# Attention into a gated feed-forward block: two matrix products interleaved, sums moved between engines

## The chip, the cores and the metric

The kernel runs on one core of a Trainium2 chip. A core has TensorE (matrix products, written to the accumulation banks called PSUM), VectorE (elementwise work), ScalarE (tabulated functions and copies), GpSimd (elementwise work on SBUF, and the issue of many transfers) and SyncE (the issue of other transfers). The engines run at the same time and wait for each other by semaphores; each works through its own instructions in the order in which they were written. The metric is the device time of one execution in microseconds.

## The reference

The inputs are q, k and v of 8 batches, 8 heads, 576 positions and a head size of 64, all in float32, and two weight matrices of 512 by 2048 and 2048 by 512. The attention pools keys and values by eight positions; the feed-forward block multiplies each hidden value by its own cosine.

```python
k_p = k.reshape(B, H, Sp, 8, D).mean(axis=3)      # Sp = 72
v_p = v.reshape(B, H, Sp, 8, D).mean(axis=3)
scores = scale * np.matmul(q, k_p.transpose(0, 1, 3, 2))
scores = scores - np.max(scores, axis=-1, keepdims=True)
attn = np.exp(scores)
attn = attn / (np.sum(attn, axis=-1, keepdims=True) + 1e-09)
x = heads_joined(np.matmul(attn, v_p))            # 4608 tokens x 512
h = x @ w_in                                      # 4608 x 2048
g = h * np.cos(h)
out = g @ w_out                                   # 4608 x 512, float32
```

## The kernel before

The 4608 tokens are worked on in nine tiles of 512, numbered t = 0 to 8, one after the other. A tile first goes **up**: eight pairs of 128 hidden columns, for each pair a bank pair of PSUM that takes eight matmuls (`up_mm`, L353), a cosine on ScalarE (L363) and a product on VectorE (L367) that writes `g_sb` and so frees the bank. From tile 1 on the pairs are taken in the order 0, 4, 1, 5, 2, 6, 3, 7, in banks 0, 2, 1, the two output banks, 0, 2, 1, 0. Then the tile goes **down**, to `out`. While it does, the attention of the next batch, b = t + 1, is computed in the gaps: scores (L233), the exponential on ScalarE (L240), the values and the row sums (L268, L295), the division on VectorE (L279, L298, L300) and transposes by SyncE's queue into `xT` (L304). A batch has 576 positions and a tile 512, so the last 64 positions of a batch (`REST`) are done in the next tile.

The down projection of tile 0 is the plain one, 64 matmuls of 512 columns (L370). From tile 1 on it is a two-by-two block scheme with seven products instead of eight (`down_products`), each of 16 matmuls of 256 columns (L431). It needs sums of parts of g, called g1 to g4 (`put_g`, L397, on VectorE, each in two halves i = 0 and 1), and sums of parts of the output weights, called w1 to w4 (`put_weights`, L387, in two halves). Two output banks take the products in turn: products 0, 2, 4 and 6 go to one (A) and 1, 3 and 5 to the other (B); in the last tile each bank is a pair in separate places. After each product VectorE reads the bank (`each`: L445 for p1, the plain copy of product 0; L447 for the sums of a bank with an earlier copy). The next product of the same bank may start only after this read. From tile 7 on (t >= B - 1) the plain copy is on ScalarE.

The eight weight sums are made once, in tile 0: w1 of half 0, and w3, w2 and w4 of half 1, on VectorE; w3, w2 and w4 of half 0 and w1 of half 1 on GpSimd (L710 and L711), behind the issue of the loads for batch 2. On GpSimd's queue these are followed by the pooling of the keys and values of batch 2, which GpSimd does by three rounds of additions (`pool_first`, L156, and `pool_rest`, L162, L165 and L168), with the loads for the batch after in between.

The order around the change is written out by hand (`manual_schedule`): the order of the lines is the order on each engine. In tile 0 a list `fill` gives pairs of a matmul number and a piece of attention that is put in front of that matmul. In later tiles the sums of g for half 0 are put between the up pairs (L580), the sums of half 1 behind the first two products (L668 and L672). At the end of a tile GpSimd waits at a gate (L714), a copy of one element of g4, before it begins the next batch's pooling.

For the first stretch of a down projection these lines give the order:

```python
product(0)
product(1, 0, 2)
scores_of(u0, u1, u2)      # three score blocks, then three exponentials
product(1, 2)
put_gs((1, 1), (2, 1))
reads[0]()                 # p1: the copy of bank A, product 0
put_gs((3, 1), (4, 1))
reads[1]()                 # bank B, product 1
values_rows(*u0)
product(2)                 # bank A again; reads g2 and w2
```

Of the kernel before, what the change touches and what calls it, by code (L numbers as in the profile page):

```python
# [20 lines left out]
def kernel(  # L21
# [377 lines left out]
    def put_gs(*kis):  # L399
        for k, i in kis:  # L400
            put_g(k, i)

    def down_products(t):

        def of(w, m=0):
            return lambda fc: w[fc // 4][:, fc % 4, m * HM:(m + 1) * HM]

        def part(x):
            return lambda fc, p: x[:, fc, p * 128:(p + 1) * 128]

        apart = t == NT - 1
        if apart:
            A, Bb = [[x[:, 0:HM] for x in two] for two in (obanks, (banks[1][:, 0, :], banks[2][:, 0, :]))]
        else:
            A, Bb = [[obanks[i][:, p * HM:(p + 1) * HM] for p in range(2)] for i in (1, 0)]
        products = [
            (A, True, part(g_part(0, 0, 0, HF)), of(w_out_sb[0:2])),
            (Bb, True, part(g_part(1, 0, 0, HF)), of(w_out_sb[2:4])),
            (A, True, part(g2), of(w2)),
            (Bb, True, part(g1), of(w1)),  # L420
            (A, False, part(g3), of(w3)),
            (Bb, False, part(g4), of(w_out_sb[2:4], 1)),
            (A, False, part(g_part(1, 1, 0, HF)), of(w4)),
        ]
        mms = []
        for n, (bank, first, g, w) in enumerate(products):
            order = [(fc, p) for fc in range(HF) for p in range(2)]
            if apart and n == 6:
                order.sort(key=lambda x: x[1])
            for fc, p in order:  # L430
                mms.append(lambda bank=bank, first=first, g=g, w=w, fc=fc, p=p: nc.tensor.matmul(  # L431
                    bank[p], lhsT=g(fc, p), rhs=w(fc),
                    start=(first and fc == 0 and (apart or p == 0)), stop=(fc == HF - 1 and (apart or p == 1)),
                    skip_group_check=not first))

        p1, v16, q15 = [msb.tile([128, 2, HM], FP32, name=n, tag=n, bufs=1) for n in ("p1_sb", "v_sb", "q_sb")]
        o1, o2 = [msb.tile([128, 2, d_model], FP32, name="o_two", tag="o_two", bufs=2) for _ in range(2)]
        m1, m2 = slice(0, HM), slice(HM, d_model)

        def each(out, bank, other=None, m=slice(0, HM), tk=None):  # L440

            for p in range(2) if apart else (slice(0, 2),):
                ps = bank[p] if apart else obanks[1 if bank is A else 0].rearrange("p (a m) -> p a m", a=2)
                if other is None:
                    (nc.scalar.copy if t >= B - 1 else nc.vector.tensor_copy)(out=out[:, p, m], in_=ps)  # L445
                else:
                    nc.vector.tensor_tensor(out=out[:, p, m], in0=ps, in1=other[:, p], op=ADD)  # L447
                if apart and tk is not None:
                    rows_out(t, tk, out, (p,), m, (nc.sync, nc.scalar))

        reads = [
            lambda: each(p1, A),
            lambda: each(o1, Bb, p1, m1, 0),
            lambda: each(v16, A, p1),
            lambda: each(q15, Bb, p1),
            lambda: each(o2, A, q15, m2, 1),
            lambda: (each(o1, Bb, v16, m2, 0), apart or stores.append(lambda: rows_out(t, 0, o1))),
            lambda: (each(o2, A, p1, m1, 1), apart or stores.append(lambda: rows_out(t, 1, o2))),
        ]
        return [mms[i * 2 * HF:(i + 1) * 2 * HF] for i in range(7)], reads  # L460
# [100 lines left out]
    for t in range(NT):  # L561
# [5 lines left out]
        for n, fp in enumerate(up_order(t)):  # L567
            up_mm(t, fp, 2 if n < 2 else 0)
            between = ()
            if t == 0:  # L570
                if fp == 4:
                    puts = pool_k_mm(1, obanks[0], 0, 2), pool_k_mm(1, obanks[1], 2, 4)
                elif fp in (5, 6):
                    g0 = 9 * (fp - 5)
                    puts = q_transpose_mm(1, obanks[0], g0, g0 + 5), q_transpose_mm(1, obanks[1], g0 + 5, g0 + 9)
                if fp in (4, 5, 6):
                    puts[0](vec)
                    between = ((puts[1], act),)
            up_g(t, fp, between)
            if 0 < t and 3 <= n < 6:  # L580
                put_gs(*[(k, 0) for k in (((3,), (1,), ()) if t == 1 else ((1, 2), (3,), (4,)))[n - 3]])
            if 0 < t and b < B:
                if n == 0:
                    q_transpose(b)
                    k_transpose(b)
                elif n == 2:
                    pool_rest(b, "v")
                    if b + 1 < B:
                        nc.gpsimd.tensor_copy(out=gate, in_=kk[b % 2][0:1, H - 1, 0:1])
                        load_q(b + 1)  # L590
                        load_kv(b + 1, "v", v)
            if n == 2:
                while stores:
                    stores.pop(0)()
# [17 lines left out]
            fill = [(1, lambda: scores(t, REST, banks[2])), (16, lambda: values(t, REST, banks[1]))]  # L612
        if t == 0:
            fill = [(2, fill[0][1]), (2, S_(0, 0)), (8, lambda: pool_v_mm(1, banks[1])),
                    (8, lambda: values(t, REST, banks[2])), (8, S_(1, 0)), (8, V_(0, 1)),
                    (18, S_(2, 2)), (21, V_(1, 0, later)), (26, S_(3, 1)), (32, lambda: later.pop()()),
                    (32, V_(2, 2)), (40, V_(3, 0))]
        if t == FIRST:
            early_inverses.clear()
# [14 lines left out]
        else:  # L634
# [21 lines left out]
            steady, rest = b < B, t < B  # L656
            if rest:
                exp_tables()
            product(0)
            product(1, 0, 2)  # L660
            if steady:
                scores_of(u0, u1, u2)
            elif rest:
                scores_of(ur)
            product(1, 2)
            if t == 1:
                put_g(2, 0)
            put_gs((1, 1), (2, 1))  # L668
            reads[0]()
            if not steady:  # L670
                reads[1]()
            put_gs((3, 1), (4, 1))  # L672
            if steady:
                reads[1]()
                values_rows(*u0)
            if t == 1:
                put_g(4, 0)
            product(2)
            reads[2]()
            if steady:  # L680
# [24 lines left out]
        if b + 1 < B:  # L705
            if t == 0:
                load_kv(b + 1, "k", k)
                load_q(b + 1)
                load_kv(b + 1, "v", v)
                put_weights(0, nc.gpsimd, (3, 2, 4))  # L710
                put_weights(1, nc.gpsimd, (1,))  # L711
            else:

                nc.gpsimd.tensor_copy(out=gate, in_=g4[0:1, HF - 1, 0:1])  # L714
            pool_first(b + 1, "k")
            if t != 1 and b + 2 < B:
                load_kv(b + 2, "k", k)
            pool_rest(b + 1, "k")
            if t == 1:
                load_kv(b + 2, "k", k)  # L720
            pool_first(b + 1, "v")
# [28 lines left out]
```

The softmax here doesn't subtract the row's maximum and nothing guards it: scores larger than these inputs give would overflow.

## Time and profile before

| What | Time |
| --- | --- |
| Five runs, median | 286.54 us |
| Five runs, lowest and highest | 285.9 and 287.77 us |
| The profiled execution | 286.72 us |
| Its span | 284.9 us |
| TensorE busy in it | 276.3 us |
| VectorE busy | 215.3 us |
| ScalarE busy | 164.4 us |
| GpSimd busy | 143.8 us |
| Mean granted TensorE clock | 1.0 of full speed |

The profile is of one execution. Its span runs from the first to the last instruction on the core; the device time around it is a little longer. A row of a timeline gives the start in microseconds, the busy time, the engine, the line of the kernel, the operation with what it writes and reads, and how many instructions were merged; a bracket at its end gives the idle time ahead of it and what ended that. Instructions of one engine overlap a little, so that ends and starts cross. PE is TensorE, DVE VectorE, ACT ScalarE, POOL GpSimd and SP SyncE.

### The profile page before, as it was taken

The numbers are of one execution on the slowest core, as the hardware profiler recorded it, in microseconds if no ns is written. First come the engines' busy times: TensorE is split into PE (matmuls) and PEld (weight loads), VectorE is DVE, ScalarE is ACT, GpSimd is POOL, SyncE is SP. The second block draws the span as 40 slices with busy tenths as digits, with TensorE's granted clock in tenths as the row PEclk, the third lists the DMA queues.
The fourth block names the chain that finished last, engine by engine and source line by source line (L and its number), as shares of the span: only waits on it lengthen the run. The fifth ranks groups of instructions, "written<-read, shape, count | busy, mean of one in ns | idle before, by whom it ended". The sixth has DMA issues, their size and how long they took to land.

```text
span 284.9 us, 5857 instructions
## 1 busy us (share of the span) xinstructions
PE 276.3 (97%) x2360; PEld 176.5 (62%) x2360; DVE 215.3 (76%) x314; ACT 164.4 (58%) x193; POOL 143.8 (50%) x150
## 2 busy tenths in 40 slices
PE   7889999999999999999999999999999999999994
PEld 2545554446874587459745884588458844874583
DVE  5448757899957995699569956995699569856972
ACT  3787798367257735674566556655656555436600
POOL 8453169997599259934993499439900000000000
PEclk9999999999999999999999999999999999999999
DMA  7999999793939698898678968882670252015014
GB/s 147 194 206 208 206 205 220 123 204 50 148 45 170 124 217 139 132 171 164 104 136 154 181 96 154 145 175 55 117 157 3 55 123 45 0 24 126 2 37 111
DMA packets 57737, 36.12 MB, mean 127 GB/s; under 512 B 35440, under 2 KB 53360, under 8 KB 57712
## 3 DMA queue, kind: packets, MB, share of 16 engines
q0 software_dynamic: 19744, 18.07, 41.1%
q1 hardware_dynamic: 37328, 17.18, 29.4%
q10 hardware_dynamic: 640, 0.52, 0.8%
q8 instruction: 18, 0.29, 0.4%
q14 instruction: 7, 0.06, 0.1%
HBM read 36.70 MB, written 9.44 MB: 162 GB/s over the span
## 4 chain that ended last, share of the span: by engine, by line
PE 86%; DVE 6%; ACT 3%; DMA 2%; issue 1%; POOL 0%; DVEq 0%; POOLq 0%; ACTq 0%
PE bank L353 35%; PE obank L431 32%; PE obank L370 4%; PE obank L353 4%; PE bank L233 3%; DVE g_sb L367 3%; DMA q_b<-in_q_dram 2%; PE bank L295 2%; PE bank L431 2%; PE bank L268 1%; DVE w L387 1%; DVE g L397 1%; ACT cos L363 1%; ACT ex L240 1%; DVE vz L187 0%
## 5 line engine op out<-in xcount | busy, mean ns | idle before, releaser
L353 PE MATMUL bank<-xT,w_in_sb 128*128 128x512 bf16 x512 | 114.0, 379 | 0.2 <-DVE g_sb L367 0.2
L363 ACT ACTIVATE cos<-bank,half_pi 128x1024 f32<-128x1024 f32 x64 | 70.4, 1114 | 56.9 <-PE bank L353 55.0
L353 PEld LDWEIGHTS <-w_in_sb 128*128 128x128 bf16 x576 | 56.1, 98 | 66.2 <-issue 0.9
L367 DVE TENSOR_TENSOR g_sb<-bank,cos 128x1024 bf16<-128x1024 f32 x64 | 77.1, 1219 | 25.1 <-ACT cos L363 24.9
L156 POOL TENSOR_TENSOR half_sums<-kv_st 72x512 f32<-72x512 bf16 x48 | 54.8, 1168 | 0.6 <-issue 0.2
L240 ACT ACTIVATE ex<-bank 72x1024 bf16<-72x1024 f32 (+1 forms) x40 | 35.0, 929 | 34.0 <-PE bank L233 33.8
L431 PEld LDWEIGHTS <-g 128*128 128x128 bf16 x512 | 47.9, 98 | 6.2 <-issue 0.3
L431 PE MATMUL obank<-w,g 128*128 128x256 bf16 x368 | 42.7, 272 | 0.2 <-DVE p_sb L445 0.2
L431 PEld LDWEIGHTS <-g_sb 128*128 128x128 bf16 x384 | 36.8, 98 | 6.9 <-DVE g_sb L367 0.3
L162 POOL TENSOR_TENSOR half_sums<-half_sums 72x512 f32<-72x512 f32 x24 | 30.5, 1290 | 0.0
L431 PE MATMUL obank<-w_out_sb,g_sb 128*128 128x256 bf16 x240 | 28.9, 273 | 0.0
L397 DVE TENSOR_TENSOR g<-g_sb 128x1024 bf16<-128x1024 bf16 x32 | 23.3, 729 | 0.5
L714 POOL COPY gate<-g 1x1 bf16<-1x1 bf16 x5 | 0.9, 181 | 34.5 <-DVE g L397 34.5
L279 DVE TENSOR_TENSOR xT<-bank,inv 64x256 bf16<-64x256 f32 x14 | 5.9, 422 | 15.0 <-ACT inv L275 14.9
L300 DVE TENSOR_TENSOR x_rows<-bank,inv_rows 128x512 bf16<-128x512 f32 x24 | 16.6, 691 | 0.8
L431 PE MATMUL obank<-w_out_sb,g 128*128 128x256 bf16 x112 | 15.6, 273 | 0.0
L431 PE MATMUL obank<-w,g_sb 128*128 128x256 bf16 x128 | 15.3, 273 | 0.0
L370 PE MATMUL obank<-w_out_sb,g_sb 128*128 128x512 bf16 x64 | 15.2, 379 | 0.0
L353 PE MATMUL obank<-xT,w_in_sb 128*128 128x512 bf16 x64 | 15.1, 379 | 0.0
L233 PE MATMUL bank<-qT,kk 64*72 64x128 bf16 (+2 forms) x288 | 12.7, 221 | 0.0
L233 PEld LDWEIGHTS <-kk 64*72 64x72 bf16 x288 | 8.9, 110 | 5.3 <-issue 3.7
L331 ACT ACT_TABLE_LOAD x9 | 11.5, 1283 | 0.9 <-PEq L734 0.8
(103 smaller groups left out, 277.5 us busy)
## 6 DMA issues: line engine op xcount, KB each, us to landing
out_dram<-o_two SPq DMA_DIRECT2D x64, 128.0 KB, 2.4
kv_st<-in_v_dram POOLq DMA_DIRECT2D x8, 576.0 KB, 11.3
kv_st<-in_k_dram POOLq DMA_DIRECT2D x7, 576.0 KB, 8.1
q_b<-in_q_dram POOLq DMA_DIRECT2D x6, 576.0 KB, 7.5
w_in_sb<-in_moe_w_in_dram POOLq DMA_DIRECT2D x4, 512.0 KB, 14.0
w_out_sb<-in_moe_w_out_dram POOLq DMA_DIRECT2D x4, 512.0 KB, 18.6
q_b<-in_q_dram POOLq DMA_DIRECT2D x4, 288.0 KB, 12.5
g_sb<-in_k_dram SPq DMA_DIRECT2D x1, 576.0 KB, 3.9
```

The source lines that it names most:

```text
L156: nc.gpsimd.tensor_tensor(out=s[:, h:h + 2], in0=x[:, h:h + 2, 0:4, :], in1=x[:, h:h + 2, 4:8, :], op=ADD)
L162: add(out=s[:, h:h + 4, 0:2, :], in0=s[:, h:h + 4, 0:2, :], in1=s[:, h:h + 4, 2:4, :], op=ADD)
L233: nc.tensor.matmul(pair[:Sp, bank, c:c + n].rearrange("p (g n) -> p g n", n=64), lhsT=kk[b % 2][half[r], key_slot(b, h0 + i, r), 0:Sp], rh ...
L240: nc.scalar.activation(out=ex[:, 0:nh * n].rearrange("p (a n) -> p a n", a=2), in_=pair[:Sp, :, 0:nh * n // 2], func=ACTF.Exp, scale=scale ...
L300: nc.vector.tensor_tensor(out=x[0:n].rearrange("p (j a d) -> p j a d", j=KCH, a=2), in0=ps[0:n, :, 0:2 * (D + 2)].rearrange("p j (a w) -> ...
L331: nc.scalar.preload_act_table_set("natural_log_exp_and_others")
L353: nc.tensor.matmul(h[j] if h is obanks else h[:, j, :], lhsT=w_in_sb[fc // 4][:, ki, (fc % 4) * 128:(fc % 4 + 1) * 128], rhs=xT[:, ki, t * ...
L363: nc.scalar.activation(out=c, in_=ps, func=ACTF.Sin, bias=half_pi[:, :1])
L367: nc.vector.tensor_mul(out=o, in0=ps, in1=c)
L370: nc.tensor.matmul(o, lhsT=g_sb[:, fc, ms * 128:(ms + 1) * 128], rhs=w_out_sb[fc // 4][:, fc % 4, :], start=(fc == 0), stop=(fc == FFCH - 1))
L397: nc.vector.tensor_tensor(out=out[:, f0:f1], in0=x, in1=y, op=op)
L431: mms.append(lambda bank=bank, first=first, g=g, w=w, fc=fc, p=p: nc.tensor.matmul(bank[p], lhsT=g(fc, p), rhs=w(fc), start=(first and fc ...
```

## The change

Four things change. In tile 0 the four weight sums that GpSimd made are now made by VectorE, in two places of the list `fill`. In tiles 1 and 2 the sums of g of half 0 come later, and so does the element of g4 at which GpSimd's gate waits. In all tiles from 1 on, the first two products are interleaved: twelve matmuls of product 0, four of product 1, the last four of product 0; then the copy p1 is made, then come the scores and the rest of product 1. And the plain copy p1 is made by ScalarE in every tile; the former line chose it only from tile 7 on.

```diff
@@ each
-                    (nc.scalar.copy if t >= B - 1 else nc.vector.tensor_copy)(out=out[:, p, m], in_=ps)
+                    nc.scalar.copy(out=out[:, p, m], in_=ps)
@@ between the up pairs
-            if 0 < t and 3 <= n < 6:
-                put_gs(*[(k, 0) for k in (((3,), (1,), ()) if t == 1 else ((1, 2), (3,), (4,)))[n - 3]])
+
+            sums = {0: {}, 1: {5: (1,), 6: (3,)}, 2: {4: (1, 2), 5: (3,)}}.get(t, {3: (1, 2), 4: (3,), 5: (4,)})
+            put_gs(*[(i, 0) for i in sums.get(n, ())])
@@ tile 0
-                    (8, lambda: values(t, REST, banks[2])), (8, S_(1, 0)), (8, V_(0, 1)),
-                    (18, S_(2, 2)), (21, V_(1, 0, later)), (26, S_(3, 1)), (32, lambda: later.pop()()),
+                    (8, lambda: values(t, REST, banks[2])),
+                    (8, lambda: put_weights(0, nc.vector, (3, 2))), (8, S_(1, 0)), (8, V_(0, 1)),
+                    (18, S_(2, 2)), (18, lambda: put_weights(0, nc.vector, (4,))),
+                    (18, lambda: put_weights(1, nc.vector, (1,))), (21, V_(1, 0, later)), (26, S_(3, 1)), (32, lambda: later.pop()()),
@@ the down projection from tile 1 on
-            product(0)
-            product(1, 0, 2)
+
+            product(0, 0, 12)
+            product(1, 0, 4)
+            product(0, 12)
+            reads[0]()
             if steady:
                 scores_of(u0, u1, u2)
             elif rest:
                 scores_of(ur)
-            product(1, 2)
+            product(1, 4)
             if t == 1:
                 put_g(2, 0)
             put_gs((1, 1), (2, 1))
-            reads[0]()
             if not steady:
                 reads[1]()
             put_gs((3, 1), (4, 1))
             if steady:
                 reads[1]()
+                if t <= 2:
+                    put_g(4, 0)
                 values_rows(*u0)
-            if t == 1:
-                put_g(4, 0)
             product(2)
@@ the end of a tile
-                put_weights(0, nc.gpsimd, (3, 2, 4))
-                put_weights(1, nc.gpsimd, (1,))
             else:
 
-                nc.gpsimd.tensor_copy(out=gate, in_=g4[0:1, HF - 1, 0:1])
+                nc.gpsimd.tensor_copy(out=gate, in_=g4[0:1, 0 if t <= 2 else HF - 1, 0:1])
```

## The prediction

> **What bounds the kernel now.** The first part of the page comes first, because it says whether any engine is full.
>
> ```profile
> PE 276.3 (97%) x2360; PEld 176.5 (62%) x2360; DVE 215.3 (76%) x314; ACT 164.4 (58%) x193; POOL 143.8 (50%) x150
> ...
> PE 86%; DVE 6%; ACT 3%; DMA 2%; issue 1%; POOL 0%; DVEq 0%; POOLq 0%; ACTq 0%
> ```
>
> TensorE is busy for 97% of the span and holds 86% of the chain that ended last. The change takes no matmul away, so it can win only the time in which TensorE waits. I looked for that by cutting the span at the first up matmul of tiles 1 to 4 (busy time by stretch; first number the length, then the busy time of each engine).
>
> ```profile
> 53.50:83.30 29.80, 29.34 (x257) 19.49 (x256) 27.07 (x35) 17.05 (x19) 24.49 (x23) 1.00 0.73 118
> 83.30:112.30 29.00, 28.97 (x257) 19.29 (x256) 23.14 (x35) 17.05 (x19) 19.99 (x21) 1.00 0.95 153
> 112.30:141.25 28.95, 28.95 (x258) 19.41 (x256) 23.01 (x35) 17.04 (x19) 19.93 (x21) 1.00 0.84 142
> ```
>
> The same work takes 29.80 us in tile 1, 29.00 in tile 2 and 28.95 in tile 3, at a granted clock of 1.00. Tile 1 loses 0.85 us and tile 2 0.05. Tile 3 has nothing to give, and neither have the tiles like it. Tile 1 is also where VectorE is fullest: 27.07 us of 29.80. The chain in order of time says how.
>
> ```profile
> 54.23 2.20 DVE w L387
> 56.45 1.65 DVE w L387
> 58.10 1.15 DVE g_sb L367
> ...
> 62.89 1.73 DVE g L397
> 64.62 1.14 DVE g_sb L367
> 65.77 0.04 issue
> 65.81 1.90 PE bank L353 x8
> ...
> 72.03 0.61 DVE p_sb L445
> 72.65 0.04 issue
> 72.69 1.91 PE obank L431 x16
> ```
>
> VectorE enters tile 1 late, behind two weight sums. The sum g3 (L397) is ahead of the product that frees bank 0, and the eight matmuls of the last up pair wait for that bank until 65.81. Later VectorE's copy p1 (L445) ends at 72.64, and the third product, which writes the copied bank, starts at 72.69. The waits themselves are 0.22 and 0.23 us; the rest of the 0.85 is restarting: the eight matmuls take 1.90 instead of 1.73, the product's sixteen 1.91 instead of 1.75.
>
> The three VectorE sums are slow beside GpSimd, whose timeline comes next.
>
> ```profile
> 38.68 2.14 POOL L387 TENSOR_TENSOR w<-w_out_sb,w_out_sb 128x1024 bf16<-128x1024 bf16 x1
> ...
> 47.27 4.93 POOL L156 TENSOR_TENSOR half_sums<-kv_st 72x512 f32<-72x512 bf16 x4
> ...
> 53.36 2.49 POOL L162 TENSOR_TENSOR half_sums<-half_sums 72x512 f32<-72x512 f32 x2
> ...
> 62.80 2.95 POOL L162 TENSOR_TENSOR half_sums<-half_sums 72x512 f32<-72x512 f32 x2
> ```
>
> The slow sums lie exactly on GpSimd's additions: 2.27 us at 54.14, 1.65 at 56.45, 1.81 at 62.81. With GpSimd idle the same shape takes 0.68 (36.22).
>
> **Part 1: the four weight sums go to VectorE in tile 0.** Removed: four GpSimd sums, 2.14 + 2.12 + 2.12 + 2.13 = 8.5 us, from 38.68 to 47.3. Added: four VectorE sums of the shape of L387, 4 x 0.68 = 2.7 us if GpSimd is idle. The first two come behind the product that ends at 40.01; VectorE then idles 1.93 us until 41.94, and 1.36 us fit. The other two come behind the product that ends at 43.33; VectorE then idles 1.34 us until the copy at 44.67, and 1.36 fit within 0.02. So on the path they cost 0 to 0.1. Without this cover the multiplication at 41.94 would be late. It frees bank 1 at 43.33, and scores on TensorE take that bank at 43.69, so there is 0.36 us of slack on top.
>
> Does GpSimd move 8.5 us earlier? Its next work is the first key sum of batch 2, and this is the DMA row for that load, issued at 26.37:
>
> ```profile
> kv_st<-in_k_dram POOLq DMA_DIRECT2D x1, 576.0 KB, 20.5
> ```
>
> It lands at 26.37 + 20.5 = 46.9. So GpSimd idles from 38.7 to 46.9 and starts only 0.4 us earlier than the 47.27 of before. That keeps it idle under all four new sums, and leaves the pair at 54.14 to 58.1 beside L162 and L165 as it is, some 0.4 us earlier. The loads of keys (52.50) and the query and value loads behind the gate move by the same 0.4 us on GpSimd's queue. The output stores and transposes on SyncE's queue wait for VectorE's copies at 44.67 and later, which do not move.
>
> The Trainium skill, "SBUF — State Buffer", section "SBUF: two separate sides", speaks against this part: a VectorE instruction with two SBUF inputs and a GpSimd instruction lock each other out for the whole instruction. Were GpSimd adding at 40 us, the four sums would by that rule wait up to one addition each, 4 x 1.16 us. The 1.81 us row fits it (wait for one addition, then work); the 2.27 us row waited through two.
>
> **Part 2: the sums of g in tiles 1 and 2 later.** In tile 1, g3 leaves the place ahead of the bank-0 product. VectorE's own order then gives: weight sums done 57.7; four products at 1.2 to 61.3, and the two halves to 62.6; the freeing product, whose cosine is ready at 62.6, from 62.65 to 63.9. TensorE wants the bank at 65.43, so the first stall goes with 1.5 us to spare. Next in line is the last up pair's product: g1 (0.68) and g3 (0.68) now lie between, the cosine is ready at 68.35, the product ends at 69.85 to 70.3 (the later if g1 meets GpSimd's last addition, which ends near 66.3). The third score block, on that bank, wants to start at 67.15 + 2.72 = 69.87. So 0 to 0.4 us of a new wait; I take 0.05. In tile 2 the sums move behind GpSimd's L168 (0.95 becomes 0.68), and the fourth moves behind the second product's read; the 0.05 us goes. GpSimd's gate in both tiles then opens near 74.1 and 103.3 instead of 73.97 and 102.89; its values are ready at 121.2 and are read after 130, so nothing follows. Without the gate this shift would put key sums beside VectorE's sums again.
>
> **Part 3: first two products interleaved in eight tiles, first bank copied by ScalarE in six more.** Twelve matmuls of product 0, four of product 1, the last four of product 0: no more matmuls, 109 ns each. The g that ends up last for product 0 is needed 4 x 0.109 = 0.44 us later. Scores come two matmuls later, 0.22 us. No row shows a return to an open bank straight from another bank's sum; the nearest is product 1's return after the scores, whose 14 matmuls take 1.63 us in the chain of tile 3 where 14 x 0.109 is 1.53. So one return more costs 0 to 0.1 a tile, 0 to 0.8 over eight tiles; I take 0, since at the plain product borders 16 matmuls keep to 1.75. VectorE loses 6 x 0.68 = 4.1 us, off the path from tile 3 on; in tile 1 the copy's end at 72.64 no longer holds product 2, for which g2 is due instead: (69.85 to 70.3) + 3 x 0.61, 71.7 to 72.1, and its second half is read only from 72.7.
>
> ScalarE gains the copy ahead of the three exponentials. The shape is in the trace:
>
> ```profile
> 244.87 0.57 ACT L445 COPY p_sb<-obank 128x512 f32<-128x512 f32 x1
> ...
> 127.29 1.28 ACT L331 ACT_TABLE_LOAD   x1
> 128.59 2.84 ACT L240 ACTIVATE ex<-bank 72x1024 bf16<-72x1024 f32 x3
> ...
> 130.47 0.41 PE L295 MATMUL bank<-vz,ex 72*128 72x65 bf16 x8
> ```
>
> In tile 3 up ends at 126.12, product 0 now at 126.12 + 20 x 0.109 = 128.3, the table load at 128.57, the copy at 129.15, the first exponential near 130.1; its reader starts on TensorE at 130.6 (the row's 130.47 overlaps the instruction before). Slack falls from about 1.0 to 0.45, and is not used up. Bounds for the copy: 0 to, with a wait of one more 0.57 us instruction, 0.1 a tile, 0.7 in all; I take 0, by the row. The copy brings no table load: at 244.87 it follows the exponential directly.
>
> **Sum.** -0.85 - 0.05 (tiles 1 and 2) + 0.05 (new wait in tile 1) + 0.05 (tile 0) = -0.8. The profiled execution took 286.72 us, span 284.9 and 1.8 around it; it becomes 285.9. It stands 0.2 above the median 286.54, so for medians 285.7; I say 285.8.
>
> **Rivals.** (A) *New wait in tile 0*, slower: the keys land earlier than 46.9, or the four sums are slow for another reason, and VectorE's multiplication is late. It decides when the first two sums take more than 1.93 + 0.36 = 2.3 us. With one key addition (L156, mean 1168 ns) ahead of each of the four, 4.6 us of delay less 2.2 us of cover and slack left over is 2.4 us on the path: 286.5 - 0.8 + 2.4 = 288.1. Against it: the landing row, in a stretch with the DMA engines full. (B) *ScalarE becomes late*, slower: the loss is 6 x (copy and its wait - 1.0). It breaks even at 1.15 us a copy; at 1.28 + 0.57 it is 6 x 0.85 = 5.1 us, 290.8. Against it: 0.57 in the row, and no reload after it. The Trainium skill, "ScalarE: Activation LUTs", section "What ACT_TABLE_LOAD costs", puts a switch at 2.66 us with its drain where the row has 1.28; by it (B) would end at 299. (C) *The stall moves instead of going*: VectorE still meets GpSimd at 54.14, and the last product of tile 1 comes at 70.3 or later; the gain is 0 to 0.3, 286.4. For it: VectorE has 27 us of work in 29.8. (D) *More is lost in unprofiled runs in tile 1 than in this execution*, whose stall hangs on where VectorE and GpSimd meet: one more collision of 1.1 us removed gives 284.7.
>
> **How the numbers follow.** A measurement of this kernel tells about 0.5% (1.4 us) from no change, so within is 285.1 to 288.0. Forecast 0.5, (A) 0.12, (B) 0.05, (C) 0.2, (D) 0.13. Faster: (D) and a little of the forecast's lower edge, 0.2. Slower: (B), half of (A) and a little for what is not seen, 0.15. Same: 0.65. The range 284.8 to 287.5 reaches (D), (C) and the light part of (A); the forecast's own is 285.2 to 286.3.
>
> **What the changed profile would show.** Tile 1's stretch near 29.0, with neither wait of TensorE in it; four VectorE rows of L387 near 0.68 between 40 and 44.7; GpSimd idle until about 46.9; six ScalarE copies of 0.57 ahead of the exponentials and no wait of the first value matmuls on them. I am wrong if TensorE waits for the multiplication in tile 0, if steady tiles exceed 28.95, or if TensorE waits for the last product of tile 1.

## The result, and the profile after

The changed kernel takes 286.15 us (median of 37 runs, 285.24 to 287.73) where the kernel before takes 286.76 (62 runs in the same comparison). The ratio is 0.9975, with a 95% interval of 0.9966 to 0.9985: about 0.7 us less. 285.8 and "within 0.5%" were forecast. The profiled execution took 286.01 us with a span of 284.2, where the one before had 284.9.

The first part of the page after, and its shares of the chain that ended last:

```profile
PE 275.5 (97%) x2360; PEld 176.3 (62%) x2360; DVE 213.4 (75%) x312; ACT 167.2 (59%) x199; POOL 133.8 (47%) x146
...
PE 90%; DVE 3%; DMA 2%; ACT 2%; issue 1%; POOL 0%; DVEq 0%; POOLq 0%; ACTq 0%
```

VectorE's share of the chain falls from 6% to 3%: the run of VectorE work at the start of tile 1 is no longer in it. Now the same cut of the span by tiles (busy time by stretch; length first, then the busy time of each engine), tiles 1 to 4 and then what follows the last matmul. The last line is that of the kernel before, for the same stretch.

```profile
53.47:82.30 28.83, 28.83 (x258) 19.38 (x256) 24.55 (x34) 17.55 (x20) 22.01 (x22) 1.00 0.70 122
82.30:111.17 28.87, 28.87 (x258) 19.41 (x256) 22.31 (x34) 17.52 (x20) 19.51 (x22) 1.00 0.96 148
111.17:140.45 29.28, 29.14 (x258) 19.33 (x256) 23.12 (x34) 17.52 (x20) 21.11 (x22) 1.00 0.92 148
140.45:169.28 28.83, 28.83 (x257) 19.32 (x256) 22.42 (x34) 17.52 (x20) 20.11 (x21) 1.00 0.82 142
...
279.62:284.20 4.58, 0.00 (x0) 0.00 (x0) 0.43 (x1) 0.00 (x0) 0.00 (x0) 0.77 0.47 106
```

```profile
280.79:284.90 4.11, 0.00 (x0) 0.00 (x0) 0.42 (x1) 0.00 (x0) 0.00 (x0) 1.00 0.52 116
```

Tile 1 goes from 29.78 to 28.83 in this execution, as was meant. But three stretches moved that the prediction had left alone. Steady tiles take 28.83 instead of 28.95. Tile 3 takes 29.28 instead of 28.94. The end takes 4.58 instead of 4.11. The experiments are mostly about these three.

In tile 0, and at the product of tile 1 that frees bank 0, VectorE's rows stand nearly where the prediction put them:

```profile
40.01 0.69 DVE L387 TENSOR_TENSOR w<-w_out_sb,w_out_sb 128x1024 bf16<-128x1024 bf16 x1
40.74 0.69 DVE L387 TENSOR_TENSOR w<-w,w_out_sb 128x1024 bf16<-128x1024 bf16 x1
41.91 1.39 DVE L279 TENSOR_TENSOR xT<-bank,q_sb 64x512 bf16<-64x512 f32 x2 [0.48 <-ACT q_sb L275]
43.33 0.69 DVE L387 TENSOR_TENSOR w<-w_out_sb,w 128x1024 bf16<-128x1024 bf16 x1
43.94 0.68 DVE L387 TENSOR_TENSOR w<-w_out_sb 128x1024 bf16<-128x1024 bf16 x1
...
63.29 1.22 DVE L367 TENSOR_TENSOR g_sb<-bank,cos 128x1024 bf16<-128x1024 f32 x1 [1.03 <-ACT cos L363]
```

```profile
46.57 4.94 POOL L156 TENSOR_TENSOR half_sums<-kv_st 72x512 f32<-72x512 bf16 x4 [7.94 <-DMA kv_st<-in_k_dram]
```

The four weight sums take 0.69 us each in two idle gaps of VectorE, the multiplication behind the first pair starts on time, and GpSimd stands idle beside them for 7.94 us, waiting for the keys to land. The product that frees bank 0 now starts at 63.29 and ends at 64.5, 0.9 us before TensorE wants the bank (65.4).

Tile 3 shows the new loss. The chain of the changed kernel, in order of time, and the GpSimd row beside it:

```profile
119.99 1.50 DVE g L397
121.49 0.02 issue
121.52 0.69 DVE g L397
122.21 1.15 DVE g_sb L367
123.35 0.04 issue
123.40 1.89 PE bank L353 x8
```

```profile
119.67 1.26 POOL L168 TENSOR_TENSOR vz<-half_sums 72x512 bf16<-72x512 f32 x1
```

The sum g1 takes 1.50 us instead of 0.69: it waits for GpSimd's last addition. The product that frees bank 0 comes behind it, and the last up pair waits for the bank. This is the picture of tile 1 before the change, two tiles later.

### The profile page after: what moved, and what is told of

Its sections match the earlier page's. It is cut to its first block, busy times and chain, and to the rows that moved or that the text cites. A ratio compares the mean times of both kernels' runs of the same rounds, so it can differ in the third digit from the quotient of the medians.

```text
span 284.2 us, 5855 instructions
## 1 busy us (share of the span) xinstructions
PE 275.5 (97%) x2360; PEld 176.3 (62%) x2360; DVE 213.4 (75%) x312; ACT 167.2 (59%) x199; POOL 133.8 (47%) x146
## 4 chain that ended last, share of the span: by engine, by line
PE 90%; DVE 3%; DMA 2%; ACT 2%; issue 1%; POOL 0%; DVEq 0%; POOLq 0%; ACTq 0%
PE bank L353 37%; PE obank L431 33%; PE obank L370 4%; PE obank L353 4%; PE bank L233 3%; DMA q_b<-in_q_dram 2%; PE bank L295 2%; PE bank L431 2%; DVE g_sb L367 2%; PE bank L268 1%; ACT ex L240 1%; ACT cos L363 1%; DVE g L397 1%; DVE vz L187 0%; PE obank L177 0%
```

## The experiments

The table has the lengths of tiles 1 to 6 (from the last matmul of one tile to that of the next, read from TensorE's timeline) and of the rest of the span from the start of the last tile, in microseconds of the profiled execution. The span is read to 0.1 us, so the rest is good to 0.05. The last two columns are the median and the ratio to the kernel before, timed in turn with it on the same chip, with its 95% interval.

| Kernel | 1 | 2 | 3 | 4 | 5 | 6 | last tile and end | median | ratio |
| --- | --- | --- | --- | --- | --- | --- | --- | --- | --- |
| before | 29.78 | 29.03 | 28.94 | 28.95 | 28.95 | 28.95 | 30.17 | 286.76 | |
| changed | 28.83 | 28.87 | 29.28 | 28.83 | 28.82 | 28.83 | 30.63 | 286.15 | 0.9975 [0.9966, 0.9985] |
| 1 weights only | 36.38 | 29.78 | 28.95 | 28.94 | 28.95 | 28.95 | 30.15 | 294.38 | 1.0277 [1.0260, 1.0294] |
| 2 sums only | 29.35 | 29.17 | 29.88 | 28.95 | 28.94 | 28.95 | 30.20 | 287.69 | 1.0037 [1.0023, 1.0051] |
| 3 interleave and copy | 29.16 | 28.83 | 28.82 | 28.83 | 28.83 | 28.82 | 30.86 | 286.14 | 0.9985 [0.9972, 0.9998] |
| 4 changed, tile 3 later | 29.40 | 28.87 | 28.87 | 29.29 | 28.82 | 28.83 | 30.84 | 286.36 | 0.9996 [0.9985, 1.0007] |
| 5 weights, gate moved | 29.46 | 30.03 | 28.94 | 28.96 | 28.94 | 28.96 | 30.17 | 287.06 | 1.0029 [1.0015, 1.0044] |
| 6 interleave, VectorE copy | 29.39 | 28.83 | 28.83 | 28.82 | 28.83 | 28.83 | 30.19 | 285.38 | 0.9967 [0.9956, 0.9978] |
| 7 changed, three copies | 29.88 | 29.87 | 29.87 | 29.87 | 29.88 | 29.86 | 30.13 | 290.93 | 1.0158 [1.0140, 1.0176] |
| 8 changed, all late | 29.22 | 28.87 | 28.88 | 28.87 | 28.88 | 28.88 | 30.73 | 285.80 | 0.9978 [0.9968, 0.9987] |
| 9 changed, VectorE copy | 29.21 | 28.87 | 29.44 | 28.82 | 28.83 | 28.83 | 30.20 | 286.20 | 0.9983 [0.9970, 0.9997] |
| 10 interleave, one ScalarE copy | 29.02 | 28.83 | 28.82 | 28.83 | 28.83 | 28.82 | 30.10 | 285.32 | 0.9960 [0.9944, 0.9977] |
| 11 changed, old gate | 29.46 | 29.04 | 30.69 | 28.82 | 28.83 | 28.83 | 30.89 | 288.41 | 1.0063 [1.0041, 1.0085] |
| 12 changed, GpSimd busy | 28.82 | 28.88 | 29.29 | 28.83 | 28.82 | 28.83 | 30.78 | 290.91 | 1.0152 [1.0130, 1.0174] |

Tile 1 began between 52.8 and 54.2 us in these executions (at 58.5 in run 12), with no order by kernel, as the first transfers landed sooner or later; a single span is therefore uncertain by more than a tile's length is. Tile 1 itself depends on this: in run 4 its instructions are those of the changed kernel, and it takes 29.40 instead of 28.83. So a difference of half a microsecond between two entries of the first column shows little.

### One part alone: the weight sums, the later sums, the interleave with the copy

The first three runs put one part each into the kernel before. Run 1:

```diff
-                    (8, lambda: values(t, REST, banks[2])), (8, S_(1, 0)), (8, V_(0, 1)),
+                    (8, lambda: values(t, REST, banks[2])),
+                    (8, lambda: put_weights(0, nc.vector, (3, 2))), (8, S_(1, 0)), (8, V_(0, 1)),
...
-                put_weights(0, nc.gpsimd, (3, 2, 4))
-                put_weights(1, nc.gpsimd, (1,))
```

> The kernel before with the four weight sums moved to VectorE and nothing else. Theory (the two waits of tile 1 come from g3 ahead of the bank-0 product and from the copy p1): GpSimd starts about 0.7 us earlier (46.6 instead of 47.3), the weight sums at the end of tile 0 finish near 57.4 instead of 58.1, but g3 then meets the next GpSimd additions (62.1 to 64.6) and both waits stay: tile 1 takes 29.4 to 29.8 us, the later tiles 28.95, the time is 0 to 0.4 us lower. Rival (the weight sums are what delays tile 1): tile 1 falls to 29.0 and the time by 0.8.

Measured: 294.38 us, 7.8 us slower, against both theories. VectorE's rows of tile 1, then GpSimd's, then TensorE's:

```profile
75.18 6.39 DVE L397 TENSOR_TENSOR g<-g_sb,g 128x1024 bf16<-128x1024 bf16 x1
```

```profile
74.10 4.48 POOL L156 TENSOR_TENSOR half_sums<-kv_st 72x512 f32<-72x512 bf16 x4
78.54 2.47 POOL L162 TENSOR_TENSOR half_sums<-half_sums 72x512 f32<-72x512 f32 x2
81.09 1.87 POOL L165 TENSOR_TENSOR ring<-half_sums 72x512 bf16<-72x512 f32 x2
```

```profile
82.22 3.37 PE L431 MATMUL obank<-w,g 128*128 128x256 bf16 x16 [5.40 <-DVE v_sb L447]
```

Six GpSimd additions follow each other without a pause. The first is just ending when the fourth sum of g for half 0 is due (0.89 us in the kernel before, at 75.19); the sum is shut out through the other five and gets through at 81.0, where GpSimd's next addition has to wait for the one in front of it. TensorE then waits 5.40 us for a bank that VectorE reads behind this sum. In the kernel before the same sum met the same additions and won after the first: GpSimd's began at 74.38 and not at 74.10. So, by these rows, 0.3 us of a shift turned a wait of 0.2 us into one of 5.7.

Run 2 has the later sums of tiles 1 and 2 and the gate's new element alone:

```diff
-            if 0 < t and 3 <= n < 6:
-                put_gs(*[(k, 0) for k in (((3,), (1,), ()) if t == 1 else ((1, 2), (3,), (4,)))[n - 3]])
+            sums = {0: {}, 1: {5: (1,), 6: (3,)}, 2: {4: (1, 2), 5: (3,)}}.get(t, {3: (1, 2), 4: (3,), 5: (4,)})
+            put_gs(*[(i, 0) for i in sums.get(n, ())])
...
```

> The kernel before with the later sums of g in tiles 1 and 2 and the gate's new element, nothing else. Theory: the wait for bank 0 goes, but TensorE then arrives earlier at the third product and waits there for the copy p1, which still ends near 72.6: tile 1 falls only to 29.4 to 29.7, tile 2 to 28.95 to 29.0, time 0.1 to 0.4 lower. Rival (the bank-0 wait is a loss of its own): tile 1 falls by the 0.4 us of that wait and its restart, to 29.35 or less.

Tile 1 takes 29.35, between the two; the waits decide for the theory, since TensorE still waits 0.2 us for the copy p1, at 73.04, and no longer for bank 0. The time went the other way: 0.37% slower, because tile 3 rises to 29.88. Its sum g1 takes 1.80 us at 121.56, beside GpSimd's L168 at 121.54.

Run 3 has the interleave and the ScalarE copy alone:

```diff
-            product(0)
-            product(1, 0, 2)
+            product(0, 0, 12)
+            product(1, 0, 4)
+            product(0, 12)
+            reads[0]()
...
-                    (nc.scalar.copy if t >= B - 1 else nc.vector.tensor_copy)(out=out[:, p, m], in_=ps)
+                    nc.scalar.copy(out=out[:, p, m], in_=ps)
```

> The kernel before with the two products interleaved and the copy p1 on ScalarE, nothing else. Theory: the wait for bank 0 in tile 1 stays (0.4), the wait for p1 goes: tile 1 takes 29.2 to 29.3. The steady tiles 4 to 6 fall from 28.95 to 28.83, because the scores start two matmuls later and no longer wait for bank 0, which the last up pair's product frees. Tile 3 is without the wait for bank 0 that the changed kernel has, or has less of it. In all 1.0 to 1.2 us lower. Rival (the 0.12 us of a steady tile come with the sums or the gate): steady tiles stay at 28.95 and the time falls by 0.5.

The tiles come out as the theory has them: 29.16, then 28.83 throughout, and no loss in tile 3. The sum of the tiles is 1.3 us lower than before, but the time is only 0.15% lower, where 1.0 to 1.2 us were expected: 0.7 us are given back between the start of the last tile and the end.

So the parts do not add up. Alone, the weights cost 7.8 us, the sums 1.1, and the interleave with the copy wins 0.5; together they win 0.7. What the moved weights bring, and what the gate has to do with it, the next runs show.

### What the moved weights bring

Run 5 adds to run 1 only that GpSimd's gate in tile 1 waits for the very sum that was shut out:

```diff
-                nc.gpsimd.tensor_copy(out=gate, in_=g4[0:1, HF - 1, 0:1])
+                nc.gpsimd.tensor_copy(out=gate, in_=g4[0:1, 0 if t == 1 else HF - 1, 0:1])
```

> The first experiment's kernel (weight sums on VectorE and nothing else), where the fourth sum of g of tile 1 took 6.39 us at 75.18 beside GpSimd's additions, with one change more: GpSimd's gate of tile 1 reads the element that this very sum writes, so that the additions begin behind it. Theory (the loss of 8 us is VectorE shut out by a row of GpSimd additions that began ahead of the sum): the sum takes 0.7 us, tile 1 falls from over 36 us to 29.6 to 29.8, the time is within 0.4 of before. Rival (the loss comes with the moved weight sums, in tile 0 or through late weights): it stays above 290.

The sum takes 0.68 us at 74.24, tile 1 29.46, and the 7.8 us are gone: the shut-out was the cause. But GpSimd's gate opens at 75.05 instead of 73.97, its last addition of tile 2 ends later, and tile 2 pays 1.0 us. VectorE's sums in tile 2 and GpSimd's addition:

```profile
91.09 0.99 DVE L397 TENSOR_TENSOR g<-g_sb 128x1024 bf16<-128x1024 bf16 x1
92.12 1.64 DVE L397 TENSOR_TENSOR g<-g,g_sb 128x1024 bf16<-128x1024 bf16 x1
```

```profile
91.61 1.60 POOL L168 TENSOR_TENSOR vz<-half_sums 72x512 bf16<-72x512 f32 x1
```

The change moves the sums of tile 2 out of the way and its gate as well, and the collision reappears in tile 3. Run 4 carries this on by one tile:

```diff
-            sums = {0: {}, 1: {5: (1,), 6: (3,)}, 2: {4: (1, 2), 5: (3,)}}.get(t, {3: (1, 2), 4: (3,), 5: (4,)})
+            sums = {0: {}, 1: {5: (1,), 6: (3,)}, 2: {4: (1, 2), 5: (3,)}, 3: {4: (1, 2), 5: (3,)}}.get(t, {3: (1, 2), 4: (3,), 5: (4,)})
...
-                if t <= 2:
+                if t <= 3:
...
-                nc.gpsimd.tensor_copy(out=gate, in_=g4[0:1, 0 if t <= 2 else HF - 1, 0:1])
+                nc.gpsimd.tensor_copy(out=gate, in_=g4[0:1, 0 if t <= 3 else HF - 1, 0:1])
```

> The changed kernel with tile 3 treated like tile 2: its sums of g one and two up pairs later, the fourth behind the second product's read, the gate on that one. Theory (g1 of tile 3 waits for GpSimd's L168, which now ends behind it, and delays the product that frees bank 0): tile 3 falls from 29.28 to 28.83 to 28.88, the span by 0.4 against the changed kernel. Rival (the wait moves on: to tile 4, or to the last product of tile 3): tile 3 or 4 keeps 0.3 us or more above 28.83, no gain.

Tile 3 falls to 28.87 and tile 4 rises to 29.29: the rival is right, the wait moves on, and nothing is won. VectorE's row of tile 4 and GpSimd's:

```profile
149.00 1.50 DVE L397 TENSOR_TENSOR g<-g_sb 128x1024 bf16<-128x1024 bf16 x1
```

```profile
148.68 1.26 POOL L168 TENSOR_TENSOR vz<-half_sums 72x512 bf16<-72x512 f32 x1
```

This execution also shows something about tile 1, where the kernel is still the changed one. Its rows of VectorE and TensorE there:

```profile
65.73 1.34 DVE L397 TENSOR_TENSOR g<-g_sb 128x1024 bf16<-128x1024 bf16 x1
```

```profile
69.99 0.41 PE L233 MATMUL bank<-qT,kk 64*72 64x128 bf16 x8 [0.38 <-DVE g_sb L367]
```

TensorE began the tile 0.4 us earlier than in the changed kernel's execution, and GpSimd's last addition came 0.5 us later (65.24 instead of 64.69). The sum g1 meets it and takes 1.34 us instead of 0.68, the last product ends at 69.93, and the third score block waits 0.38 us for its bank. In the changed kernel's execution that product ended at 69.71, less than 0.2 us ahead of the block.

The loss of the later tiles sits in the first tile whose sums keep the early place behind a tile whose gate opened late. Run 8 uses the late places in all tiles:

```diff
-            sums = {0: {}, 1: {5: (1,), 6: (3,)}, 2: {4: (1, 2), 5: (3,)}}.get(t, {3: (1, 2), 4: (3,), 5: (4,)})
+            sums = {0: {}, 1: {6: (1,), 7: (3,)}}.get(t, {4: (1, 2), 5: (3,)} if t < 7 else {3: (1, 2), 4: (3,), 5: (4,)})
...
-                if t <= 2:
-                    put_g(4, 0)
+                put_g(4, 0)
...
-                nc.gpsimd.tensor_copy(out=gate, in_=g4[0:1, 0 if t <= 2 else HF - 1, 0:1])
+                nc.gpsimd.tensor_copy(out=gate, in_=g4[0:1, 0, 0:1])
```

> The changed kernel with the late places for the sums of g and the gate in all tiles 2 to 6, and in tile 1 one up pair later still. Theory (what is left above 28.83 in tiles 1 to 6 is sums of g that meet GpSimd's last addition): tiles 1 to 6 all take 28.8 to 28.9, 0.4 to 0.5 less than the changed kernel in all; the span goes to 283.7. Rival (the later sums come too late for the third product, or the later gate makes GpSimd late): some tile takes 29.1 or more, and nothing is won.

Tiles 2 to 6 take 28.87 to 28.88, so no collision is left in them. Tile 1 takes 29.22, though, over the 29.1 that the rival named; this execution began it 0.5 us early, and VectorE's chain of tile 1 ends little earlier for that. The ratio, 0.9978, is that of the changed kernel.

Run 11 takes the changed kernel and gives its gate the old element again in tiles 1 and 2, with the fourth sum left behind the second product's read:

```diff
-                nc.gpsimd.tensor_copy(out=gate, in_=g4[0:1, 0 if t <= 2 else HF - 1, 0:1])
+                nc.gpsimd.tensor_copy(out=gate, in_=g4[0:1, HF - 1, 0:1])
```

> The changed kernel with GpSimd's gate on the element of before in tiles 1 and 2, so that its key additions begin ahead of the fourth sum of g, which stays behind the second product's read. Theory (the sum can be shut out by a row of additions): in tile 1 or 2 the sum takes 1.2 us (waits for the running addition) to 7 us (waits for the whole row), and the time is 0.3 to 8 us higher; tile 3 is at 28.83, since GpSimd's last addition of the tile ends earlier. Rival (the first experiment's 6.39 us had another cause): both sums take 0.7 to 0.9 and the time falls by 0.4.

Both sums now take 1.46 us: they wait for the rest of one addition, not for the row. Tile 3 missed the expectation, with 30.69. VectorE meets nobody there; TensorE waits at the start of the tile, and the trace puts that down to an instruction that was long done. TensorE's row, the transpose into `xT` (the input of the up projection) on SyncE's queue with the time to its landing, and the key load on GpSimd's queue:

```profile
113.21 5.34 PE L353 MATMUL bank<-xT,w_in_sb 128*128 128x512 bf16 x24 [1.70 <-DVE o_two L447]
```

```profile
107.06 1.22 SPq L304 DMA_TRANSPOSE xT<-x_rows  x1
...
DMA to landing us min/median/max: 5.9/5.9/5.9
```

```profile
107.00 0.84 POOL L115 DMA_DIRECT2D kv_st<-in_k_dram  x1 [0.30 <-POOL half_sums L156]
```

The third transpose lands at 107.06 + 5.9 = 113.0, and TensorE goes on at 113.21. In the changed kernel the key load is issued at 107.59, behind the third transpose (106.47), and that transpose lands after 3.0 us. The changed kernel has the bad order once too, in tile 3: the third transpose is issued at 135.74, 0.08 us behind a key load, and lands after 6.0 us; tile 4 needs only the first two and does not wait. So an earlier gate also puts a load in front of a transpose that the next tile needs. That the load is what held the transpose is argued from these places; no run moved the load alone.

### The interleave and the copy

Run 6 is run 3 with the copy left on VectorE:

```diff
-                    nc.scalar.copy(out=out[:, p, m], in_=ps)
+                    (nc.scalar.copy if t >= B - 1 else nc.vector.tensor_copy)(out=out[:, p, m], in_=ps)
```

> The kernel before with the two products interleaved, the copy p1 still on VectorE, but now ahead of the second-half sums of g. Theory (the steady tiles win because the scores start two matmuls later and do not wait for bank 0): tiles 4 to 6 take 28.83 as in the third experiment, and the copy's engine is worth nothing in them. Tile 1 keeps the bank-0 wait, 29.2 to 29.3. Rival (the win of the steady tiles comes with the copy on ScalarE): tiles 4 to 6 stay at 28.95.

Tiles 4 to 6 take 28.83, so the steady gain comes with the interleave and not with the copy's engine. Tile 1 takes 29.39, a little over what was expected: VectorE, with the copy in it, is late there once more, and TensorE waits 0.33 us for its read of the third product. The steady gain can be seen in the score blocks. Tile 4 before, the product that frees bank 0, then the third block of scores, which takes that bank; then all three blocks in the chain, in tiles 2 and 4 before and in tile 4 of the changed kernel:

```profile
156.25 1.23 DVE L367 TENSOR_TENSOR g_sb<-bank,cos 128x1024 bf16<-128x1024 f32 x1 [0.16 <-ACT cos L363]
```

```profile
157.53 0.41 PE L233 MATMUL bank<-qT,kk 64*72 64x128 bf16 x8
```

```profile
99.26 0.79 PE bank L233 x24
...
157.03 0.91 PE bank L233 x24
```

```profile
156.44 0.79 PE bank L233 x24
```

Before, the product ends at 157.48 and the third block starts at 157.53, behind a gap; the 24 matmuls take 0.91 us in the chain. After, the blocks run through in 0.79, since they start two matmuls later in the tile. That is the 0.12 us.

Run 7 makes the ScalarE copy three times:

```diff
-                    nc.scalar.copy(out=out[:, p, m], in_=ps)
+                    for _ in range(3 if t < B - 1 else 1):
+                        nc.scalar.copy(out=out[:, p, m], in_=ps)
```

> The changed kernel with the ScalarE copy p1 made three times in a row in tiles 1 to 6. In tile 4 of the changed kernel the first exponential ends at 158.23 and its reader on TensorE starts at 158.65: slack 0.42. Theory (ScalarE has that slack and no more): two more copies add 0.98 to 1.16 us, the reader waits 0.56 to 0.74 a tile, 28.83 becomes 29.4 to 29.6 and the time rises by 3.3 to 4.5 us. Rival (there is more slack behind the first reader): under 1 us in all.

ScalarE's rows of tile 4 with three copies, and TensorE's:

```profile
159.00 1.82 ACT L446 COPY p_sb<-obank 128x512 f32<-128x512 f32 x3
160.72 2.84 ACT L240 ACTIVATE ex<-bank 72x1024 bf16<-72x1024 f32 x3
```

```profile
161.79 0.42 PE L295 MATMUL bank<-vz,ex 72*128 72x65 bf16 x8 [0.87 <-ACT ex L240]
```

The three copies take 1.82 us, 1.24 more than one. The wait of 0.87 is more than the 0.56 to 0.74 expected, because the two copies cost 0.62 us each where 0.49 to 0.58 was expected; 1.24 less the slack of 0.42 is 0.82. The tile grows by 1.04: the wait and its restart. So the slack is about what it was read to be, and one copy leaves 0.4 us of it.

### The end of the span

Run 9 undoes only the copy's engine in the changed kernel:

> The changed kernel with one part undone: the copy p1 on VectorE again in tiles 1 to 6. Seen so far: from the last tile's start to the end of the span takes 30.1 to 30.2 us in all kernels with that copy on VectorE and in the one with three copies, and 30.6 to 30.9 in all with one copy on ScalarE; there an instruction transfer falls into the last stores. Theory (the six more instructions of ScalarE move that transfer to the end): the last stretch is back at 30.1 to 30.2, 0.45 less than the changed kernel; tiles 4 to 6 stay at 28.83; tile 1, where VectorE is full, takes 0.1 to 0.6 more. The time is within 0.3 of the changed kernel. Rival (the end differs by something else, the interleave or the sums): it stays at 30.6 or more.

The last stretch is back at 30.20; tile 1 is 0.38 longer, which by run 4 shows little, and tile 3 0.16. All fourteen kernels fit: the six with six ScalarE copies more than before (changed, runs 3, 4, 8, 11 and 12) have a long end, with one transfer on an instruction queue in the last 3 us or so, and the others have a short end and no such transfer in the last 5 us. The transfers of the last 5 us, changed kernel first, then run 9:

```profile
q14 instruction: 1, 0.01, 0.8%
...
out_dram<-o_two SPq DMA_DIRECT2D x3, 64.0 KB, 2.0
out_dram<-o_two ACTq DMA_DIRECT2D x3, 64.0 KB, 2.3
```

```profile
out_dram<-o_two SPq DMA_DIRECT2D x3, 64.0 KB, 2.0
out_dram<-o_two ACTq DMA_DIRECT2D x3, 64.0 KB, 2.1
```

ScalarE's queue issues half of the last stores. In the changed kernel its last one starts 0.38 us behind the end of the one before (279.73 + 0.55, then 280.66), in the kernel before 0.09 us (280.89 + 0.58, then 281.56). The last store on SyncE's queue is issued 0.49 us behind the last matmul in both kernels, but takes longer to land; changed kernel, then before:

```profile
DMA to landing us min/median/max: 2.6/2.6/2.6
```

```profile
DMA to landing us min/median/max: 2.0/2.0/2.0
```

Run 7, with twelve ScalarE instructions more than the changed kernel, has its instruction transfer some 10 us before the end, and a short end of 30.13. So six copies more on ScalarE bring an instruction transfer among the last stores, and 0.45 us of what the tiles won go there. The dependence of the end on the count of ScalarE instructions is shown. That the transfer slows the landing of the last stores is argued from where it lies. It is not what made ScalarE's issue late: it begins at 281.38, behind that issue. What did stays open.

Run 10 takes the interleave and one ScalarE copy, in the one tile in which VectorE is full, and nothing else of the change:

```diff
-                    nc.scalar.copy(out=out[:, p, m], in_=ps)
+                    (nc.scalar.copy if t == 1 or t >= B - 1 else nc.vector.tensor_copy)(out=out[:, p, m], in_=ps)
```

> The kernel before with the two products interleaved and the copy p1 on ScalarE in tile 1 only (and from tile 7 on, as before); weights, sums and gate as before. Theory: tile 1, the one in which VectorE is full, falls from 29.39 in the sixth experiment to 29.0 to 29.2, tiles 2 to 6 take 28.83, the last stretch 30.1 to 30.2: span 283.7, 0.3 less than the sixth and 0.5 less than the changed kernel. Rival (one instruction more is enough to bring the instruction transfer into the end): last stretch 30.6 or more and no gain over the sixth.

All as expected: 29.02, 28.83 and 30.10, and the span is 283.4, even lower than the 283.7 expected. With 285.32 us and a ratio of 0.9960 it is the lowest of all kernels, next to run 6 with 0.9967. Both intervals are clear of 1; they overlap with the changed kernel's, so that these are better than the changed kernel rests on their spans and on the stretches in the table. By these, the weight sums, the later sums of g and the gate can be left out.

### GpSimd busy beside the weight sums

Run 12 gives GpSimd four additions of the same shape at the old place, into a tile that nobody reads:

```diff
+                for x in (w_out_sb[0], w_out_sb[2], w_out_sb[0], w_out_sb[2]):
+                    nc.gpsimd.tensor_tensor(out=spare, in0=x[:, :, 0:HM], in1=x[:, :, HM:], op=ADD)
...
```

> The changed kernel with four additions of the same shape given to GpSimd at the old place, into a tile that nobody reads, so that GpSimd is busy from 38.7 to 47.3 while VectorE makes the four weight sums. This is the case that the prediction's rival (A) priced. Theory: a VectorE sum waits for the addition that runs, up to 2.1 us, or for the row; the first two end past 42.3, the multiplication behind them is late, TensorE waits for bank 1: the down projection of tile 0 ends 1 to 6 us later. Rival (short instructions share the port well enough): the sums take 0.7 to 1.0, and the time is within 0.4 of the changed kernel.

VectorE's rows, then TensorE's:

```profile
39.62 1.33 DVE L388 TENSOR_TENSOR w<-w_out_sb,w_out_sb 128x1024 bf16<-128x1024 bf16 x1
40.99 2.50 DVE L388 TENSOR_TENSOR w<-w,w_out_sb 128x1024 bf16<-128x1024 bf16 x1
43.52 1.39 DVE L280 TENSOR_TENSOR xT<-bank,q_sb 64x512 bf16<-64x512 f32 x2
44.94 1.08 DVE L388 TENSOR_TENSOR w<-w_out_sb,w 128x1024 bf16<-128x1024 bf16 x1
45.94 2.60 DVE L388 TENSOR_TENSOR w<-w_out_sb 128x1024 bf16<-128x1024 bf16 x1
```

```profile
44.97 0.41 PE L234 MATMUL bank<-qT,kk 64*72 64x256 bf16 x4 [1.21 <-DVE xT L280]
...
49.32 2.68 PE L371 MATMUL obank<-w_out_sb,g_sb 128*128 128x512 bf16 x8 [2.11 <-DVE o_two L376]
```

TensorE waits twice: at the place named, for the bank that the late multiplication frees, and then for the output bank that VectorE copies behind the second pair. The last matmul of tile 0 ends at 58.5 instead of 53.5, and from tile 1 on all stretches are those of the changed kernel. The time rises by about 5 us over the changed kernel's (4.8 between the medians, 5.2 between the spans). So the idle gap of GpSimd, which came from the late landing of the keys, is what made the moved sums free.

## Why the prediction was right

The total was right: -0.8 forecast, -0.6 to -0.7 measured. In the profiled execution tile 1 went as forecast. Elsewhere terms that were not seen nearly cancel, so that the total comes this close is in part luck.

- **Weight sums on VectorE.** 0.69 us each, in the two gaps named, with no delay behind them. GpSimd started at 46.57 where 46.9 was forecast, 0.7 us earlier than before and not 8.5: the landing row of the key load was the right row to ask. The price put on tile 0 (0.05) was not paid.
- **The shut-out.** The text took a VectorE sum to wait for one GpSimd addition, at most two. Run 1 shows five. The Trainium skill, "SBUF — State Buffer", section "SBUF: two separate sides", has the loser blocked for the whole instruction; an estimate by it is a wait for one addition, of 1.16 us here, and run 1's wait of 5.7 us is five times that. In the changed kernel the gate keeps the additions behind the sum, as part 2 said in one sentence with no price. With the weights alone moved, runs 1 and 5 put the price at about 7 us; in run 11, the changed kernel with the old gate, the sums met the rest of one addition only.
- **Tile 1.** Forecast 29.0, measured 28.83. The freeing product stood at 62.65 to 63.9 in the text and at 63.29 to 64.5 in the trace, both ahead of 65.43; the last product ended at 69.7. No new wait, where 0.05 was allowed, but less than 0.2 us was left: in run 4 the same instructions have TensorE wait 0.38 us for the last product, and tile 1 takes 29.40. That is the top of the 0 to 0.4 in the text, the picture of rival (C), and one of its signs of being wrong; how often it happens in the executions without a profile is not recorded. Nor is the gain of tile 1 shown to need parts 1 and 2: runs 3 and 10, which leave the weights and the sums as before, have it at 29.16 and 29.02. (On the way, three products of 1.2 us lie between 57.7 and 61.3, not four; the time given is right.)
- **"So nothing follows."** This step failed: the later gate in tile 2 was judged by who reads what GpSimd computes, after 130 us. It costs 0.45 us in tile 3 through whom GpSimd's additions hold up, and tile 3 at 29.28 is over the 28.95 that the text named as a sign of being wrong. Runs 2, 4, 5 and 9 show that collision in tiles 2, 3 and 4, wherever a tile with early sums follows a late gate.
- **Interleave at 0 in steady tiles.** Failed by 0.12 us a tile. "Tile 3 has nothing to give" was read off the busy share of TensorE, 28.95 of 28.95. A gap of a tenth inside overlapping rows does not show there; the score block's 0.91 us in the chain, against 0.79 for the same block in tile 2 of the same profile (at 99.26), would have shown it.
- **The ScalarE copy.** 0.58 us for 0.57, slack 0.42 for 0.45, no table load, no wait. Rival (B)'s formula, six times the copies less 1.0, gives 4.9 us for run 7's 1.82 us of copies, and its median is 4.8 over the changed kernel's. That they agree is luck in part: a tile grows by 1.04 and not by 0.82, and the short end gives 0.5 back. What the text had not seen is that six instructions more cost 0.45 us at the end.
- **Rival (A)** has the right place and the right point of decision: the first two sums took 3.9 us in run 12, over the 2.3 named. Its price, 2.4 us where tile 0 ended 5.0 later, is not tested by this run: the text priced additions of 1.17 us, and those of run 12 take 2.1 or more; and it left out that the second pair holds up the output copy as well.

Summed over the profile: -0.95 in tile 1, -0.16 in tile 2, +0.34 in tile 3, three times -0.12, +0.46 at the end, and 0.04 less in front: -0.7, the difference of the spans.

## What to carry to other kernels

When an engine shares a port with another, price a moved instruction by what runs beside it at that moment, and ask of every instruction that becomes later whom it will now hold up, not only who waits for its result. In a kernel whose bound engine shows no idle time, the same block in two places, or with two neighbours, tells small waits that the busy share hides. And try each part of a composite change alone: here the interleave wins in tiles 1 to 6, and the gate mends what the moved weights break.

## What was not expected of the hardware

- A VectorE sum with two SBUF inputs (0.68 us alone) beside a row of GpSimd additions waited for part of one (1.46 us at 72.97 in run 11), for one (1.81 at 62.81 in the kernel before), through two (2.27 at 54.14), or through five (6.39 at 75.18 in run 1). In the two long cases it got through where GpSimd's next addition read what the one in front of it had just written and GpSimd paused for some 0.1 us. What decides between a win after one addition and a wait to the next pause stays open; 0.3 us of shift were enough to turn it.
- Six instructions added to ScalarE early in the program came with an end longer by 0.45 us and with an instruction transfer in it; with twelve more both were gone.
- In run 11, a transpose issued on SyncE's queue 0.06 us behind a 576 KB load on GpSimd's took 5.9 us to land; 3.0 us in the changed kernel, where it goes 1.1 us ahead of the load.
